# A squared-ReLU MLP whose last 96 hidden units move from three matmuls a tile to two and a packed quarter

## The chip, the cores and the metric

The kernel runs on one core of a Trainium2 chip. The metric is the device time of one execution in microseconds. Engines are named as in the profile: PE is TensorE (PEld its weight loads), DVE VectorE, ACT ScalarE, POOL GpSimd, and SP is SyncE, which here only issues transfers (its queue shows as SPq).

## The reference

One block of a transformer with two branches in parallel on 2048 tokens of 512 features, in float32:

```python
x = A_x                                   # [1, 2048, 512]
xn = layernorm(x)                         # no weights
# A: linear attention, 32 heads of 16
q, k, v = (xn @ wqkv) split into heads    # wqkv [512, 1536]
phi = lambda t: where(t > 0, t + 1, exp(t)) + 1e-6
kv = einsum("bhsd,bhse->bhde", phi(k), v) # over all tokens, not causal
z = einsum("bhsd->bhd", phi(k))
o = einsum("bhqd,bhde->bhqe", phi(q), kv) / (phi(q) . z + 1e-6)
A = o @ wo                                # wo [512, 512]
# B: an MLP of 1376 hidden units
h = relu(xn @ w1 + b1) ** 2               # w1 [512, 1376]
B = h @ w2 + b2                           # w2 [1376, 512]
return x + A + B
```

The 1376 hidden units are ten chunks of 128 and a last one of 96. That last chunk, number 10, is what the change is about.

## The kernel before

**Numbers.** TensorE multiplies operands in a rounded format (`fp32r`). To keep float32 accuracy every operand is held as a pair: the rounded value, called high, and the rest, called low, which is the difference between the value and its high part. ScalarE writes the high part with a copy (L109), VectorE subtracts for the low part (L117, L120). A product of two pairs is three matmuls into one accumulator, high·high, high·low and low·high: the helper `three`, whose matmul is L128, goes through

```python
PASSES = ((0, 0), (0, 1), (1, 0))
```

**Tokens.** 2048 tokens are 16 tiles of 128, in four blocks of four tiles. All tiles are read once for the layer norm, the keys and the attention sums. Then two pairs of blocks are worked, n = 0 (blocks 3 and 2) and n = 1 (blocks 1 and 0). `t1` is the first block of a pair, `t2` the second.

**A pair of blocks.** The hidden units of chunks 0 to 9 are made in pairs of chunks, for both blocks at once, by a scheme with seven products in place of eight (`product`, L453), in steps p = 0 to 4 and a closing one, p = 5. Chunk 10 stands alone: `plain_1` computes it for block `t1` ahead of step 0 and for block `t2` inside step 0. The hidden values of `t1` are used while the steps run: `mlp_2` (L457) multiplies the hidden values of a chunk, 128 tokens at a time, with the rows of `w2` of that chunk, three matmuls a tile, into four PSUM accumulators `acc`. The hidden values of `t2` are kept in the tiles `r2a` to `r2c` and used after the steps, in "the second block" (L1036 to L1095). `add_attention` adds the attention's product with `wo` for one tile (`aTsr`, `aTsra` are pairs of the transposed attention result, made by a transpose `at` on VectorE, L285, from `g`, which transfers have regrouped in memory). `add` (L903) then adds the accumulator on VectorE to `res`, the rows of `x` loaded by `load_res` (L893), and `store` writes the result out.

**Chunk 10 and b2.** Chunk 10 has 96 rows of `w1` columns and `w2` rows. `raw_1` (L175) and `piece_2` (L193) fill the other 32 by a memset on GpSimd, and `b2` is loaded as row 96 of the `w2` tile. The bias `b1` of unit 96 is 1 and its weights are 0, so its hidden value is 1 and `b2` enters through the matmul that has to be done anyway. In the first block of a pair chunk 10 is the first to enter `acc` (step 0); in the second it is one of `last_two`, the two chunks whose products come after the attention's (`sum_2`, L998). The last tile of all is done in two halves of 256 columns, `end`, so that its sum and store can begin earlier.

**Order.** The order is written by hand (`manual_schedule`): the instructions of each engine run in the order in which the program names them. An instruction that waits holds all that stands behind it on its engine. All transfers are issued by SyncE in program order as well: one whose buffer is not free yet, or whose source is not written yet, holds those behind it. Loads of weights go into a ring of six raw buffers of 128x512 float32 (`raw`), from which ScalarE and VectorE make the pairs. The same ring holds the temporary sums `S1` and `S3` of `chunk_sums` (L696 to L705).

`piece_2` issues the load and returns two pieces of work, the copy and the subtraction, which `next_2` (L871) or `do(w2next, 2)` puts in later; `next_2` keeps the `w2` of the next chunk one step ahead. In the second block, the loop over the chunks (L1036) runs over nine chunks, e = 0 to 8; at e it multiplies chunk `waiting[e]`, makes the hidden pair for a later one (`wait_for`, L994), puts in the pieces of `w2` loaded before and loads the `w2` of `waiting[e + 8]`, so that chunk 10, the last in `waiting`, is loaded at e = 2, just ahead of `load_res(t2)`. At e = 3, in the pair n = 0 alone, a megabyte of normalised tokens for the next pair is loaded (`xt`, L1043); then come the `wqkv` rows for the next queries (`rq`, L162; their pairs `wrh`, `wrl`). Between them `move(4)` issues the transfers `g` that regroup the attention result.

Of the kernel before, what the change touches and what calls it, by code (L numbers as in the profile page):

```python
# [13 lines left out]
P = 128  # L14
# [4 lines left out]
def kernel(  # L19
# [46 lines left out]
    assert D == 512 and S % BT == 0 and FL % 32 == 0 and FL < P  # L66
# [79 lines left out]
    ident = keep.tile([P, P], F32, name="ident")  # L146
    heads = work.tile([P, P], F32, name="heads", tag="heads")
    b1s = keep.tile([P, NF], F32, name="b1s")
    zb = keep.tile([P, D], F32, name="zb")
# [10 lines left out]
    def raw(name, src):  # L160
        t = w512(name, "raw", 6)
        nc.sync.dma_start(t[:, :src.shape[-1]], src)  # L162
        return t
# [10 lines left out]

    def raw_1(f):  # L175
        n = min(P, F - f * P)
        t = w512(f"r1_{f}", "raw", 6)
        tj = t.rearrange("p (j n) -> p j n", j=NJ)
        if n < P:
            nc.gpsimd.memset(tj[:, :, n:], 0.0)  # L180
        nc.sync.dma_start(tj[:, :, :n], w1[:, f * P:f * P + n].rearrange("(j p) n -> p j n", j=NJ))
        return t
# [10 lines left out]
    def piece_2(f, at):  # L193

        if f < NF - 1:
            t = raw(f"r2_{f}", w2[f * P:(f + 1) * P, :])
        else:
            t = w512(f"r2_{f}", "raw", 6)
            nc.gpsimd.memset(t[FL:, :], 0.0)  # L199
            nc.sync.dma_start(t[:FL, :], w2[f * P:, :])  # L200
            nc.sync.dma_start(t[FL:FL + 1, :], b2[None, :])
        w2s[f] = [w2r[at // 2][:, at % 2 * 2 + u] for u in range(2)]
        h, l = w2s[f]
        return [lambda: copy("act", h, t), lambda: rest_of(l, t, h)]
# [234 lines left out]

    def relu(o, i, f):  # L440
# [16 lines left out]
    def mlp_2(acc, f, s, first=False):  # L457
        for k in range(TB):
            three(acc[k], [s[:, u, k * P:(k + 1) * P] for u in range(2)], w2s[f], first, False)

# [31 lines left out]
    nc.gpsimd.memset(b1s[:, NF - 1:], 0.0)  # L492
    nc.gpsimd.memset(b1s[FL:FL + 1, NF - 1:], 1.0)
# [126 lines left out]
    def less_last(j):  # L620
        if j == 0:
            nc.sync.dma_start(wvs, wqkv[:, 2 * D:].rearrange("(j p) d -> p j d", j=NJ))
            w = w512("wvl", "raw", 6)
# [23 lines left out]
    for i in range(2, NT):  # L647
        if i == NPE:
            wq = both("wq", ("B0", "B1"))
        if i == 3:  # L650
            nc.sync.dma_start(b1s[:, :NF - 1], b1[:(NF - 1) * P].rearrange("(f p) -> p f", p=P))
            nc.sync.dma_start(b1s[:FL, NF - 1:], b1[(NF - 1) * P:, None])
# [43 lines left out]
    def chunk_sums(n, t):  # L696

        (a11, a12), (a21, a22) = ((x[:, 0], x[:, 1]) for x in t)
        sa, sb = (w512(f"S{k}_{n}", "raw", 6).rearrange("p (c n) -> p c n", c=2) for k in (1, 3))
# [90 lines left out]
    for n in range(2):  # L790
# [76 lines left out]
        s = {NF - 1: hidden_2(f"sz{n}", rz)}  # L867
# [23 lines left out]
        t5, res = None, {}  # L891

        def load_res(t):  # L893
            for k in range(2):
# [3 lines left out]
                for i in range(2):  # L898
                    res[t, 2 * k + i] = r[:, i, :]

# [8 lines left out]
        for p in range(NP + 1):  # L909
# [6 lines left out]
            if p:  # L916
                nc.vector.tensor_tensor(out=t5, in0=before, in1=t5, op=OP.add)
            if 0 < p < NP:
                chunk_split(1, 0, s34)
            if p:  # L920
                relu(r2[fb - 2], t5, fb - 2)
            if p < NP:
# [22 lines left out]
            if p == 0:  # L945
                T.update({k: tokens_sum(k, f"B{k - 3}") for k in (3, 4)})
                def last_sums(k):
                    for f in (difference_high, difference_low):
# [3 lines left out]
                last_sums(3)  # L952
# [5 lines left out]
            else:  # L958

                plain_1(before, z, x2)  # L960
                relu(r2[NF - 1], before, NF - 1)
            s[fa] = hidden_2(f"s{n}_{fa}", c11)
# [4 lines left out]
            if p + 2 < NP:  # L967
                w = load_1(p + 2)
            product(A, S2, [T[2][:, u] for u in range(2)])
# [9 lines left out]
            if p == 0:  # L979
                last_sums(4)  # L980
            relu(r2[fa], c12, fa)
            next_2(2 * p + 2)
            if p:
                mlp_2(acc, fb - 2, s.pop(fb - 2))
            else:
                mlp_2(acc, NF - 1, s.pop(NF - 1), True)
# [49 lines left out]
        for e, f in enumerate(waiting[:-2]):  # L1036
# [28 lines left out]
        for k in range(TB):  # L1065
            add_attention(acc, t2 * TB + k, n == 1 and k == last)
# [47 lines left out]
```

## Time and profile before

The median of three runs is 422.51 us (422.31 to 422.54).

| | |
|---|---|
| profiled execution, its own time | 422.49 us |
| its span in the trace | 420.8 us |
| TensorE busy | 415.2 us, 99% of the span, 1860 matmuls |
| VectorE busy | 294.2 us, 70%, 536 instructions |
| ScalarE busy | 254.0 us, 60%, 451 instructions |
| GpSimd busy | 27.6 us, 7%, 50 instructions |
| transfers | 46.16 MB, mean 110 GB/s |
| granted TensorE clock | 1.000 |
| 128x512 matmul, mean duration in the records | 389 ns |

A row of the groups of instructions names the line, the engine, the operation, the output and the inputs by their names in the program, the shape, and the count; then busy time and mean duration of one, and the idle time of the engine just ahead of such instructions with what ended most of it. Matmuls are pipelined, so the durations of neighbours overlap: 1860 matmuls of up to 389 ns fit into 415 us. GpSimd works in the first quarter of the span, apart from a few small memsets. The 40 slices of the page show TensorE at 9 tenths or more from the second slice to the last but one, with the granted clock at full throughout.

### The profile page before, as it was taken

Reading aid. Unit: us, or ns where it says so; the run is one execution under the profiler, and the core shown is the slowest. Engines: PE = TensorE matmul, PEld = TensorE weight load, DVE = VectorE, ACT = ScalarE, POOL = GpSimd, SP = SyncE. Lnnn points to the kernel's source line nnn. Section 1 sums busy time; section 2 is a strip of 40 time slices with the busy share of each in tenths; the row PEclk is TensorE's granted clock in tenths of the full one; section 3 lists DMA queues with packets and bytes.
Section 4 is the critical chain, followed back from the end, with each engine's and each line's share of the span. In section 5 each row is a group of like instructions: output and inputs, shape, how many; then the busy total and the mean of one; then the engine's idle time right before and its main releaser. Section 6 shows DMA issues by size and latency. Waiting matters only on the chain.

```text
span 420.8 us, 5373 instructions
## 1 busy us (share of the span) xinstructions
PE 415.2 (99%) x1860; PEld 343.6 (82%) x1860; DVE 294.2 (70%) x536; ACT 254.0 (60%) x451; POOL 27.6 (7%) x50
## 2 busy tenths in 40 slices
PE   7999999999999999999999999999999999999996
PEld 7788888888887888888888888888888888888885
DVE  6886767777578877677579475586967667577343
ACT  5867777675467767665457362676667665546230
POOL 3242222220000000000000000000000000000000
PEclk9999999999999999999999999999999999999999
DMA  7885422800412231645026652401120654024502
GB/s 240 286 243 157 130 89 92 278 15 3 112 50 77 75 100 26 199 82 169 0 85 191 173 196 97 124 0 50 51 75 25 202 101 149 2 95 97 152 0 100
DMA packets 44818, 46.16 MB, mean 110 GB/s; under 512 B 5716, under 2 KB 31060, under 8 KB 44536
## 3 DMA queue, kind: packets, MB, share of 16 engines
q1 hardware_dynamic: 44792, 45.84, 36.5%
q8 instruction: 14, 0.23, 0.2%
q14 instruction: 12, 0.10, 0.1%
HBM read 32.71 MB, written 8.91 MB: 99 GB/s over the span
## 4 chain that ended last, share of the span: by engine, by line
PE 98%; DVE 1%; DMA 1%; ACT 0%; issue 0%
PE acc L128 39%; PE b L453 23%; PE kx L380 10%; PE pk L361 10%; PE pq L361 10%; PE pz L128 1%; PE b L128 1%; PE pkv L773 1%; PE pm L128 1%; DMA x<-in_A_x_dram 1%; PE pt L300 1%; PE end L128 0%; DVE st L214 0%; DVE xp L253 0%; DVE res L903 0%; ACT xs1h L316 0%
## 5 line engine op out<-in xcount | busy, mean ns | idle before, releaser
L128 PE MATMUL acc<-w2r,s 128*128 128x512 f32 x498 | 116.6, 389 | 0.0
L128 PEld LDWEIGHTS acc<-w2r,s 128*128 128x128 f32 x498 | 93.5, 188 | 19.6
L453 PE MATMUL b<-T,aop 128*128 128x512 f32 x240 | 59.6, 389 | 0.0
L453 PEld LDWEIGHTS b<-T,aop 128*128 128x128 f32 x240 | 45.0, 188 | 9.4
L380 PE MATMUL kx<-pk,tok 128*128 128x512 f32 x192 | 46.8, 392 | 0.0
L380 PEld LDWEIGHTS kx<-pk,tok 128*128 128x128 f32 x192 | 35.6, 188 | 7.9 <-DVE pk L369 0.6
L128 PE MATMUL acc<-mh,aTsr 128*128 128x512 f32 x96 | 30.3, 390 | 0.0
L109 ACT ACTIVATE w2r<-r 128x512 fp32r<-128x512 f32 x32 | 20.0, 625 | 13.8 <-PE acc L128 11.3
L120 DVE TENSOR_TENSOR w2r<-r,w2r 128x512 fp32r<-128x512 f32 x32 | 21.9, 685 | 7.3 <-ACT w2r L109 7.2
L453 PE MATMUL b<-xs0h,aop 128*128 128x512 f32 x80 | 26.4, 391 | 0.0
L117 POOL TENSOR_TENSOR tok<-xp,tok 128x512 fp32r<-128x512 f32 x16 | 21.7, 1362 | 54.9 <-ACT tok L109 54.9
L117 DVE TENSOR_TENSOR s<-c,s 128x512 fp32r<-128x512 f32 x20 | 13.8, 692 | 16.3 <-ACT s L109 16.3
L356 DVE SCALAR_TENSOR_TENSOR q<-pq,q 128x512 f32<-128x512 f32 x16 | 11.0, 689 | 14.9 <-ACT q L354 14.9
L109 ACT ACTIVATE aop<-S 128x512 fp32r<-128x512 f32 x20 | 12.6, 629 | 14.6 <-DVE S L702 9.4
L128 PEld LDWEIGHTS acc<-mh,aTsr 128*128 128x128 f32 x96 | 18.0, 188 | 3.8
L903 DVE TENSOR_TENSOR res<-acc,res 128x512 f32<-128x512 f32 x16 | 11.0, 692 | 14.2 <-PE acc L128 14.2
L352 ACT ACTIVATE q<-pq 128x512 f32<-128x512 f32 x16 | 9.4, 591 | 18.5 <-PE pq L361 18.5
L199 POOL MEMSET r<- 32x512 f32 x3 | 1.6, 522 | 278.2 <-DVE w2r L120 272.3
L128 PE MATMUL acc<-ml,aTsr 128*128 128x512 f32 x48 | 18.7, 390 | 0.0
L453 PEld LDWEIGHTS b<-xs0h,aop 128*128 128x128 f32 x80 | 15.0, 188 | 3.4 <-ACT rz L441 0.3
L453 PE MATMUL b<-xs0l,aop 128*128 128x512 f32 x40 | 15.6, 389 | 0.0
L285 DVE STREAM_TRANSPOSE at<-g 128x512 f32<-128x512 f32 x16 | 10.5, 689 | 6.8 <-DMA g<-q 6.8
(192 smaller groups left out, 826.7 us busy)
## 6 DMA issues: line engine op xcount, KB each, us to landing
r<-in_B_w_dram SPq DMA_DIRECT2D x49, 256.0 KB, 3.2
res<-in_A_x_dram SPq DMA_DIRECT2D x8, 512.0 KB, 5.9
g<-q SPq DMA_DIRECT2D x64, 64.0 KB, 2.1
out_dram<-res SPq DMA_DIRECT2D x15, 256.0 KB, 2.1
x<-in_A_x_dram SPq DMA_DIRECT2D x5, 512.0 KB, 5.6
via<-xp SPq DMA_DIRECT2D x5, 512.0 KB, 2.6
xg<-via SPq DMA_DIRECT2D x20, 128.0 KB, 3.0
xTd<-t SPq DMA_DIRECT2D x8, 256.0 KB, 3.1
```

Of the source, the lines that this page charges most:

```text
L109: nc.scalar.activation(o, i, AF.Copy, bias=bias)
L117: ENG[el].tensor_tensor(out=l, in0=src, in1=f32(h), op=OP.subtract)
L120: nc.vector.tensor_tensor(out=l, in0=src, in1=f32(h), op=OP.subtract)
L128: nc.tensor.matmul(ps, lhsT=a[u], rhs=b[v], start=first and n == 0, stop=last and n == 2)
L285: nc.vector.transpose(o.rearrange("p j (r t) -> p r j t", r=NJ), G.rearrange("p r (j c) -> p r j c", j=NJ))
L300: nc.tensor.transpose(t[k][:, at:at + P], xp[i][:, j * P:(j + 1) * P], ident)
L352: nc.scalar.activation(p, ps, AF.Relu, scale=-1.0)
L356: nc.vector.scalar_tensor_tensor(p, ps, 0.0, p, op0=OP.max, op1=OP.add)
L361: nc.tensor.matmul(ps, lhsT=cols(i)[u][:, j, slot(i)], rhs=w[v][:, j, :], start=first and n == 0, stop=last and n == len(steps) - 1)
L380: nc.tensor.matmul(kxp[c], lhsT=tok[i][:, u, c * P:(c + 1) * P], rhs=pk[i][:, v], start=i == 0 and (u, v) == first, stop=i == NT - 1 and ( ...
L453: nc.tensor.matmul(ps, lhsT=a[u][:, j * P:(j + 1) * P], rhs=b[v][:, j, :], start=first and j == 0 and n == 0, stop=last and j == 1 and n == 2,
L903: nc.vector.tensor_tensor(out=r[:, a:z], in0=ps, in1=r[:, a:z], op=OP.add)
```

## The change

Chunk 10's 96 units are laid out over 128 rows. `units(f)` says which: rows 0 to 63 hold units 32 to 95 of the chunk, and rows 64 to 95 and 96 to 127 both hold units 0 to 31. High and low parts of different units then share a tile, so that two matmuls of 128 rows (`last_2`) cover all but one 32-row product per token tile, and that one is done for the four tiles of a block together (`quarters_2`): four matmuls of 32 rows, each in another quarter of the rows of the array and into another accumulator. `b2` no longer has a row; GpSimd's queue adds it to `res` by accumulating transfers (`add_bias`).

What else moves: in the pair n = 0, step 0, the subtractions for chunk 10's hidden part stand later (`sz_rests`), and the last one of `T`'s pieces and a `next_2` move into step 1; the ring has five raw buffers, not six; in the second block chunk 10's load stands at e = 3, behind `load_res(t2)`, the `g` transfers of that step and, in the pair n = 0, `xt`; the two `wait_for` at the end of the second block change places. On GpSimd the memsets are gone, and copies of 64x512 and 32x512 come in their place. SyncE issues three transfers for each chunk-10 load.

```diff
     w2s, wos = {}, {}
-    ident = keep.tile([P, P], F32, name="ident")
+    ident = keep.tile([P, P], F32, name="ident", tag="ident")
     heads = work.tile([P, P], F32, name="heads", tag="heads")
     b1s = keep.tile([P, NF], F32, name="b1s")
-    zb = keep.tile([P, D], F32, name="zb")
+    w2q = keep.tile([P, D], F32R, name="w2q")
+    zb = work.tile([P, D], F32, name="zb")
     eps = keep.tile([P, 1], F32, name="eps")
...
     def raw(name, src):
-        t = w512(name, "raw", 6)
+        t = w512(name, "raw", 5)
         nc.sync.dma_start(t[:, :src.shape[-1]], src)
...
+    def units(f):
+        if f < NF - 1:
+            return [(0, f * P, P)]
+        return [(0, f * P + Q, 2 * Q), (2 * Q, f * P, Q), (3 * Q, f * P, Q)]
     def raw_1(f):
-        n = min(P, F - f * P)
-        t = w512(f"r1_{f}", "raw", 6)
+        t = w512(f"r1_{f}", "raw", 5)
         tj = t.rearrange("p (j n) -> p j n", j=NJ)
-        if n < P:
-            nc.gpsimd.memset(tj[:, :, n:], 0.0)
-        nc.sync.dma_start(tj[:, :, :n], w1[:, f * P:f * P + n].rearrange("(j p) n -> p j n", j=NJ))
+        for a, o, n in units(f):
+            nc.sync.dma_start(tj[:, :, a:a + n], w1[:, o:o + n].rearrange("(j p) n -> p j n", j=NJ))
         return t
...
+        h, l = w2s[f] = [w2r[at // 2][:, at % 2 * 2 + u] for u in range(2)]
         if f < NF - 1:
             t = raw(f"r2_{f}", w2[f * P:(f + 1) * P, :])
-        else:
-            t = w512(f"r2_{f}", "raw", 6)
-            nc.gpsimd.memset(t[FL:, :], 0.0)
-            nc.sync.dma_start(t[:FL, :], w2[f * P:, :])
-            nc.sync.dma_start(t[FL:FL + 1, :], b2[None, :])
-        w2s[f] = [w2r[at // 2][:, at % 2 * 2 + u] for u in range(2)]
-        h, l = w2s[f]
-        return [lambda: copy("act", h, t), lambda: rest_of(l, t, h)]
+            return [lambda: copy("act", h, t), lambda: rest_of(l, t, h)]
+        t = w512(f"r2_{f}", "raw", 5)
+        for a, o, n in units(f):
+            nc.sync.dma_start(t[a:a + n], w2[o:o + n, :])
+        def high():
+            copy("act", h, t)
+            copy("pool", l[2 * Q:], h[:2 * Q])
+            for k in range(TB):
+                copy("pool", w2q[k * Q:(k + 1) * Q], h[2 * Q:3 * Q])
+        def low():
+            rest_of(l[:2 * Q], t[:2 * Q], h[:2 * Q])
+            rest_of(h[3 * Q:], t[3 * Q:], h[3 * Q:])
+        return [high, low]
...
+    def hidden_last(name, r):
+        nc.scalar.activation(r, r, AF.Square)
+        s = pair(name)
+        h, hl = s[:, 0], s[:, 1]
+        lq = keep.tile([P, P], F32R, name=f"{name}q", tag="ident")
+        copy("act", h, r)
+        copy("pool", hl[:2 * Q], h[:2 * Q])
+        def rests():
+            rest_of(hl[2 * Q:], r[:2 * Q], h[:2 * Q])
+            for k in range(TB):
+                at, to = slice(2 * Q, 3 * Q), slice(k * P, (k + 1) * P)
+                rest_of(lq[k * Q:(k + 1) * Q], r[at, to], h[at, to])
+        return (h, hl, lq), rests
     def relu(o, i, f):
...
+    def last_2(ps, k, s, first, stop, a=0, z=D):
+        for u in range(2):
+            nc.tensor.matmul(ps, lhsT=s[u][:, k * P:(k + 1) * P], rhs=w2s[NF - 1][u][:, a:z],
+                             start=first and u == 0, stop=stop and u == 1)
+    def quarters_2(acc, s):
+        for k in range(TB):
+            at = slice(k * Q, (k + 1) * Q)
+            nc.tensor.matmul(acc[k], lhsT=s[2][at], rhs=w2q[at], start=False, stop=False)
     def add_attention(acc, i, last=False):
...
                                 channel_multiplier=sign)
-    nc.gpsimd.memset(b1s[:, NF - 1:], 0.0)
-    nc.gpsimd.memset(b1s[FL:FL + 1, NF - 1:], 1.0)
     groups = {}
...
             nc.sync.dma_start(b1s[:, :NF - 1], b1[:(NF - 1) * P].rearrange("(f p) -> p f", p=P))
-            nc.sync.dma_start(b1s[:FL, NF - 1:], b1[(NF - 1) * P:, None])
+            for a, o, n in units(NF - 1):
+                nc.sync.dma_start(b1s[a:a + n, NF - 1:], b1[o:o + n, None])
         move()
...
         (a11, a12), (a21, a22) = ((x[:, 0], x[:, 1]) for x in t)
-        sa, sb = (w512(f"S{k}_{n}", "raw", 6).rearrange("p (c n) -> p c n", c=2) for k in (1, 3))
+        sa, sb = (w512(f"S{k}_{n}", "raw", 5).rearrange("p (c n) -> p c n", c=2) for k in (1, 3))
         for o, x, y, op in ((sa[:, 0], a21, a22, OP.add), (sa[:, 1], sa[:, 0], a11, OP.subtract),
...
         relu(rz, ps, NF - 1)
-        s = {NF - 1: hidden_2(f"sz{n}", rz)}
+        sz, sz_rests = hidden_last(f"sz{n}", rz)
+        s = {}
+        if n:
+            sz_rests()
...
         r2 = {f: r2[k // 4][:, k % 4] for k, f in enumerate(waiting)}
-        t5, res = None, {}
+        t5, res, biased = None, {}, []
...
                     res[t, 2 * k + i] = r[:, i, :]
+                biased.append(r)
+        def add_bias():
+            def to(r):
+                for i in range(2):
+                    nc.gpsimd.dma_start(r[:, i], b2[None, :].partition_broadcast(P), accum_op=OP.add)
+            todo = [lambda r=r: to(r) for r in biased]
+            biased.clear()
+            return todo
...
                 nc.vector.tensor_tensor(out=t5, in0=before, in1=t5, op=OP.add)
+            if p == 1:
+                last_sums(4, difference_low)
             if 0 < p < NP:
...
                 relu(r2[fb - 2], t5, fb - 2)
+            if p == 1:
+                next_2(2)
             if p < NP:
...
                 T.update({k: tokens_sum(k, f"B{k - 3}") for k in (3, 4)})
-                def last_sums(k):
-                    for f in (difference_high, difference_low):
+                def last_sums(k, *what):
+                    for f in what:
                         for j in range(2):
...
-                last_sums(3)
+                last_sums(3, difference_high, difference_low)
             if p or n:
...
                 relu(r2[NF - 1], before, NF - 1)
+                if n == 0:
+                    sz_rests()
             s[fa] = hidden_2(f"s{n}_{fa}", c11)
...
                 w = load_1(p + 2)
+            if p == NP - 1:
+                do(bias, 2)
             product(A, S2, [T[2][:, u] for u in range(2)])
...
             if p == 0:
-                last_sums(4)
+                last_sums(4, difference_high)
             relu(r2[fa], c12, fa)
-            next_2(2 * p + 2)
             if p:
+                next_2(2 * p + 2)
                 mlp_2(acc, fb - 2, s.pop(fb - 2))
             else:
-                mlp_2(acc, NF - 1, s.pop(NF - 1), True)
+                for k in range(TB):
+                    last_2(acc[k], k, sz, True, False)
+                quarters_2(acc, sz)
             if p == TB - 1:
...
                 load_res(t1)
+            if p == 3:
+                bias = add_bias()
         def wait_for(f):
-            s[f] = hidden_2(f"s{n}_{t2}_{f}", r2[f])
+            name = f"s{n}_{t2}_{f}"
+            if f < NF - 1:
+                s[f] = hidden_2(name, r2[f])
+            else:
+                s[f], rests = hidden_last(name, r2[f])
+                rests()
         def sum_2(acc, k, f, first, stop, a=0, z=D):
+            if f == NF - 1:
+                last_2(acc, k, s[f], first, stop, a, z)
+                return
             three(acc, [s[f][:, u, k * P:(k + 1) * P] for u in range(2)],
...
                 do(w2next, 2)
-                if e + 8 < NF:
-                    g = waiting[e + 8]
+                k = e + 8 if e < 2 else e + 7
+                if k < NF and e != 2:
+                    g = waiting[k]
                     w2next.extend(piece_2(g, place(g)))
...
                 load_res(t2)
+            if e == 4:
+                bias = add_bias()
+            if e in (6, 7):
+                do(bias)
             if 0 < e < 5:
...
         for k in range(TB):
+            if n == 1 and k == last:
+                quarters_2(acc, s[NF - 1])
             add_attention(acc, t2 * TB + k, n == 1 and k == last)
             if k < 2:
-                wait_for(last_two[k])
+                wait_for(last_two[1 - k])
                 pieces(1)
...
             add(acc[last], t2, last)
+        else:
+            quarters_2(acc, s[NF - 1])
         for k in range(TB):
```

More of the change, by code (lines that the diff above doesn't have):

```diff
@@ L65 @@
     FL = F - (NF - 1) * P
-    assert D == 512 and S % BT == 0 and FL % 32 == 0 and FL < P
+    Q = P // TB
+    assert D == 512 and S % BT == 0 and FL == 3 * Q
     nc.scalar.preload_act_table_set("natural_log_exp_and_others")
@@ L622, in less_last @@
             nc.sync.dma_start(wvs, wqkv[:, 2 * D:].rearrange("(j p) d -> p j d", j=NJ))
-            w = w512("wvl", "raw", 6)
+            w = w512("wvl", "raw", 5)
             nc.sync.dma_start(w, wqkv[D - 1:, 2 * D:].partition_broadcast(P))
```

## Prediction

> **What bounds the kernel now.** I read the page first, then the chain in order of time, then who waits for whom, then the timelines around the places that the diff touches.
>
> ```profile
> span 420.8 us, 5373 instructions
> ...
> PE 415.2 (99%) x1860; PEld 343.6 (82%) x1860; DVE 294.2 (70%) x536; ACT 254.0 (60%) x451; POOL 27.6 (7%) x50
> ```
>
> The span, and each engine's busy time. The chain that ended last, by engine:
>
> ```profile
> PE 98%; DVE 1%; DMA 1%; ACT 0%; issue 0%
> ```
>
> Two rows of the groups of instructions (count, busy time, mean ns of one, idle time ahead of them):
>
> ```profile
> L128 PE MATMUL acc<-w2r,s 128*128 128x512 f32 x498 | 116.6, 389 | 0.0
> L128 PEld LDWEIGHTS acc<-w2r,s 128*128 128x128 f32 x498 | 93.5, 188 | 19.6
> ```
>
> TensorE carries 98% of the chain, so a matmul removed is time won, unless TensorE then waits. A matmul's 389 ns overlap their neighbours'; what one costs is its pitch, from the chain in order of time (start, length, engine, output, line, how many):
>
> ```profile
> 138.19 2.72 PE acc L128 x12
> ```
>
> 512 columns: 2.72/12 = 0.2267 us a matmul. At the very end, 256 columns, 1.44/12 = 0.120:
>
> ```profile
> 416.03 1.44 PE end L128 x12
> ```
>
> And 128 columns, with a new weight tile for each:
>
> ```profile
> 108.36 3.57 PE pkv L773 x32
> ```
>
> 3.57/32 = 0.1116; that is the closest row to the pace of weight loads.
>
> **The change, part by part.**
>
> *Matmuls.* The last chunk costs three matmuls for each of 16 token tiles; now two. The last tile is done in two halves, so what goes is 15 × 0.2267 + 2 × 0.120 = 3.64 us. Four groups of four 32-row matmuls come in, each of the four in its own row group, with its own 128-column weight load and 512 columns. No row shows one. Lower bound of a group: all four stream together, 0.227. Upper bound in a dense stream: one after the other, 4 × 0.2267 = 0.907, at which removing and adding cancel (3.64 − 3.63). I take the pace of `pkv` for the loads: the first is hidden under the matmul ahead as every load is now, three more take 3 × 0.1116, then the last streams its 0.2267: 0.56 a group, 2.25 in all. Gain 3.64 − 2.25 = **1.39** (ends 2.73 and 0.01; with drains, below, a loss).
>
> The Trainium skill (TensorE: Matmul & The Clock Gate, Part 3: Packing small matmuls) reports 3.07 times for four row tiles of 512 columns; by it a group would be 0.907/3.07 = 0.30 and the gain 2.46, an estimate.
>
> *The first block's start.* Chunk 10's two subtractions on VectorE (hidden and weights) become seven: the weights' two at once, the hidden part's 64-row one and four 32x128 ones later, after `T`.
>
> ```profile
> 131.52 0.68 DVE L117 TENSOR_TENSOR sz<-rz,sz 128x512 fp32r<-128x512 f32 x1
> 135.20 1.30 DVE L120 TENSOR_TENSOR T<-Tf,T 128x512 fp32r<-128x512 f32 x2 [1.20 <-ACT T L109]
> 138.03 2.88 PE L128 MATMUL acc<-w2r,sz 128*128 128x512 f32 x12
> ```
>
> And, from further on, a VectorE instruction of half the columns:
>
> ```profile
> 183.58 0.42 DVE L702 TENSOR_TENSOR S<-r,S 128x256 f32<-128x256 f32 x1
> ```
>
> Fewer rows save nothing, the columns count: the weights' pair takes two slots of 0.6 there. Behind `T` (136.5) come 0.60 for the 64 rows and some 0.25 for each quarter (the last row has 256 columns in 0.42, the first 512 in 0.68): 137.1 and 138.1. TensorE wants the first at 138.26 and the quarters after eight matmuls, at 139.8. That leaves 1.1 us against GpSimd, which now copies (next part). Price 0 to 1.2; I take 0.3.
>
> *GpSimd copies.* Five copies for each weight load of chunk 10 and one for each hidden part replace the memsets. Without a row of their own they lie between a 512-column memset and a two-input subtraction:
>
> ```profile
> L117 POOL TENSOR_TENSOR tok<-xp,tok 128x512 fp32r<-128x512 f32 x16 | 21.7, 1362 | 54.9 <-ACT tok L109 54.9
> L199 POOL MEMSET r<- 32x512 f32 x3 | 1.6, 522 | 278.2 <-DVE w2r L120 272.3
> L117 DVE TENSOR_TENSOR wql<-rq,wqh 128x512 fp32r<-128x512 f32 x4 | 4.0, 1044 | 0.6 <-ACT wqh L109 0.6
> L120 DVE TENSOR_TENSOR w2r<-r,w2r 128x512 fp32r<-128x512 f32 x32 | 21.9, 685 | 7.3 <-ACT w2r L109 7.2
> ```
>
> And from the timelines of GpSimd and VectorE (start, length, operation, in brackets the idle time ahead and what ended it), where the two meet:
>
> ```profile
> 73.57 1.33 POOL L117 TENSOR_TENSOR tok<-xp,tok 128x512 fp32r<-128x512 f32 x1 [4.06 <-ACT tok L109]
> 74.05 2.01 DVE L117 TENSOR_TENSOR wql<-rq,wqh 128x512 fp32r<-128x512 f32 x2 [0.30 <-ACT wqh L109]
> ```
>
> Two VectorE subtractions that met a GpSimd subtraction took 2.01 instead of some 1.3; `wql` averages 1044 ns where its like take 685. So GpSimd off the path still delays VectorE, by up to its own remaining time.
>
> *b2 by transfers.* Sixteen accumulating transfers on GpSimd's queue, 256 KB each, take the place of a row that cost no matmul. They follow `res` loads, many microseconds ahead of the additions; GpSimd's program order, not TensorE, times them. I cost them at nothing, except where they meet other transfers below.
>
> *Five raw buffers for six.* Loads now wait for a later release; the worst in both block pairs is `r2_8`, which waits for the last chunk sums (the row at 183.58, above) and stands ahead of 16 `g` transfers.
>
> ```profile
> 179.34 10.95 SPq L281 DMA_DIRECT2D g<-q  x16
> 197.20 0.62 ACT L109 ACTIVATE w2r<-r 128x512 fp32r<-128x512 f32 x1
> 199.85 0.73 ACT L441 ACTIVATE r2a<-c,b1s 128x512 f32<-128x512 f32 x1 [2.02 <-DVE c L977]
> 202.75 1.29 DVE L285 STREAM_TRANSPOSE at<-g 128x512 f32<-128x512 f32 x2
> ```
>
> The `g` issues move from 179.3–190.3 to about 184.5–195.5, and land some 2 us later, still ahead of 202.75. `r2_9`, queued behind them, comes some 1.3 us late for ACT's copy at 197.2, which has 2.02 idle behind it. Cost 0; if the cover went, ACT would be that late.
>
> *The second block's last weights: the decisive edit.* SyncE's queue issued chunk 10's weights ahead of `res`. Now they stand behind `xt`, a megabyte, in the same queue. `xt` itself waits until all `g` have landed.
>
> ```profile
> 232.32 0.53 SPq L200 DMA_DIRECT2D r<-in_B_w_dram  x1
> 233.24 0.90 SPq L897 DMA_DIRECT2D res<-in_A_x_dram  x2
> 234.19 2.55 SPq L281 DMA_DIRECT2D g<-q  x4
> 240.88 0.35 SPq L1043 DMA_DIRECT2D xt<-xTd  x1
> 241.33 2.06 SPq L162 DMA_DIRECT2D rq<-in_A_wqkv_dram  x4
> ```
>
> These are SyncE's issues (start, length of issuing, line, output and source, how many). Then ScalarE, VectorE and TensorE in the same stretch:
>
> ```profile
> 242.81 0.62 ACT L109 ACTIVATE w2r<-r 128x512 fp32r<-128x512 f32 x1
> 244.90 0.63 ACT L109 ACTIVATE aTsr<-at 128x512 fp32r<-128x512 f32 x1 [1.47 <-DVE at L285]
> 246.42 0.63 ACT L109 ACTIVATE wrh<-rq 128x512 fp32r<-128x512 f32 x1 [0.89 <-DMA rq<-in_A_wqkv_dram]
> 248.43 0.63 ACT L109 ACTIVATE aTsr<-at 128x512 fp32r<-128x512 f32 x1 [1.38 <-DVE at L285]
> 248.97 0.61 ACT L109 ACTIVATE wrh<-rq 128x512 fp32r<-128x512 f32 x1
> ```
>
> ```profile
> 243.56 0.68 DVE L120 TENSOR_TENSOR w2r<-r,w2r 128x512 fp32r<-128x512 f32 x1
> 244.16 0.70 DVE L285 STREAM_TRANSPOSE at<-g 128x512 f32<-128x512 f32 x1
> 247.08 0.69 DVE L117 TENSOR_TENSOR wrl<-rq,wrh 128x512 fp32r<-128x512 f32 x1 [2.22 <-ACT wrh L109]
> 247.69 0.71 DVE L285 STREAM_TRANSPOSE at<-g 128x512 f32<-128x512 f32 x1
> 248.32 1.47 DVE L120 TENSOR_TENSOR aTsr<-at,aTsr 128x512 fp32r<-128x512 f32 x2
> ```
>
> ```profile
> 250.15 0.62 PE L128 MATMUL acc<-mh,aTsr 128*128 128x512 f32 x2
> ```
>
> ACT's copy of the chunk-10 weights (242.81) stands in both orders ahead of `aTsr`, and VectorE's subtraction ahead of the transpose `at`; the attention matmul at 250.15 needs their low half, ready today near 248.97. Now the load takes the place of the first `rq`, which ended ACT's wait at 246.42, or 5.54 after `xt`'s issue. Two issues fewer ahead of `res` bring `xt` 0.92 forward (232.32 to 233.24); the accumulating transfers that start when `res` has landed hold it back by 0 to 1.4 (512 KB beside what is still under way). I take 0.6: `xt` at 240.6, weights at **246.1** (ends 245.5, 247.0) instead of long before 242.81.
>
> From there by the rows' distances: subtraction +0.75, its new second half +0.60, transpose +0.60, `aTsr` +0.74, `wrh` +0.54 (ACT's spacing of copies, 248.43 to 248.97), `wrl` +0.66, second transpose +0.61, low half +0.63, its length 0.69: 5.82, so 251.9. With some 0.25 for the weight load the matmul of 250.15 starts at 252.2: a stall of 2.0. The five GpSimd copies start with the same event and hold VectorE by 0 to 0.85; I take 0.4. **Stall 2.4** (ends 1.4 and 3.8). The last block has no `xt`, and its weights come in time.
>
> *Sum.* −1.39 + 0.3 + 2.4 = +1.3. The profiled execution took 422.49 (420.8 span, 1.7 around), beside a median of 422.51: **423.8**.
>
> **Rivals.**
>
> *Hidden, and faster.* If the chunk-10 weights land by about 244 (the 16 engines serving small transfers beside `xt` rather than behind it), the stall is under the gain; with no stall at all, 422.49 − 1.39 = 421.1. The turning point is a landing near 244.7 to 245.2. Against it: `rq`, in the same place, ended its wait only at 246.42.
>
> *The row groups do not run side by side.* Then a group costs 0.907, nothing is won, and the stalls stay: 422.49 + 2.7 = 425.2. The change would not do what it says.
>
> *Drains.* Entering and leaving a 32-row group, TensorE might run empty: the tail 0.389 − 0.227 = 0.16, a bare load 0.188, three more at 0.1116, a whole matmul 0.389, a bare load 0.188: 1.26 a group, 5.04 for 3.64: 1.4 lost, and 426.6 with the stalls. No matmul in the trace changes its row count, so no row speaks for or against. The Trainium skill (TensorEngine Tiling (Array Packing), Tiling Modes, Key Properties) says that changing the tiling mode drains TensorE; no run shown so far bears on that.
>
> **How the numbers follow.** About 0.2% (0.85 us: 421.65 to 423.35) is what tells a change from none. Stall larger than gain, as summed: 0.60, own range 422.8 to 425.4, of it 0.13 within 0.2%. Hidden: 0.22, of it 0.15 faster. No packing: 0.10, of it 0.01 within. Drains: 0.08. So slower 0.64, same 0.21, faster 0.15. The range reaches from the hidden case (421.1) to near the drain case: 421.1 to 426.2; what lies outside is the lower end of the hidden case and the upper part of the drains.
>
> **What would show it.** Matmul count unchanged at 1860 less 17 plus 16, 1859. Four groups reading `w2q`: starts within 0.12 of each other and 0.56 to the next full matmul prove the packing; 0.227 apart the second rival; gaps of 0.35 ahead of and behind them the drains. In the wait view ACT's `w2r` waits 2 to 4 us for a transfer near 246, and TensorE for `aTsr` around 250. If TensorE is still 99% busy with no such wait, the stall was wrong; if TensorE waits near 138 for `sz`, the first block's price was too small.

## The result and the profile after

The changed kernel takes 429.37 us (median of five runs, 429.19 to 430.79), the kernel before 422.54 beside it: 1.0161 times as long, 95% interval 1.0135 to 1.0186. Forecast was 423.8, in a range of 421.1 to 426.2. The direction was right, the size was not, and the time lies outside the range.

The profiled execution of the changed kernel took 430.79 us, the slowest of the five, with a span of 429.1. Its page:

```profile
span 429.1 us, 5471 instructions
...
PE 418.5 (98%) x1859; PEld 343.1 (80%) x1859; DVE 304.1 (71%) x555; ACT 253.7 (59%) x451; POOL 54.8 (13%) x78
...
PEclk9999999999999999999999987999999999999999
```

TensorE's busy time rose by 3.3 us with one matmul fewer, and the row of the granted clock, all 9s before, has an 8 and a 7 in two slices past the middle, around 260 us. TensorE's waits:

```profile
PE acc L129 <- ACT aTsr L110: 2.5, 1, 2.5
PE acc L129 <- DVE aTsr L121: 2.1, 1, 2.1
...
PE acc L500 <- DVE sz L121: 0.8, 1, 0.8
```

(us in total, times, longest). The two waits for `aTsr` are at the place that the prediction named, and the one for `sz` is in the first block. The chain in order of time shows how the delay grew. Its rows of before at three marks (a full step after the first block, the queries behind the second block, the last addition), then of after:

```profile
155.87 6.80 PE b L453 x30
...
260.79 21.76 PE pq L361 x96
...
417.50 0.42 DVE res L903
```

```profile
157.00 6.80 PE b L489 x30
...
269.39 21.76 PE pq L379 x96
...
425.62 0.42 DVE res L964
```

The delay is 1.13 after the first block, 8.60 after the second, and 8.12 at the last addition; 0.2 more at the very end makes the 8.3 between the spans. So the first block lost 1.13, the second block of n = 0 lost 7.47, and the two blocks of n = 1 together won 0.48. The changed kernel profiled a second time (429.65 us, `after_again` below) has the first two marks at 156.36 and 268.28: there the first block lost 0.49 and the second 7.00. The sizes that follow are those of one execution, the slower of the two.

**The second block of n = 0.** First the end of the chain that leads to the second wait (start, length, what):

```profile
241.92 7.58 DMA r<-in_B_w_dram
...
249.66 0.64 ACT w2r L110
...
251.03 1.01 DVE w2r L121
...
253.97 1.07 DVE wrl L118
...
256.29 3.78 PE acc L129 x8
```

In full this is the forecast path link by link: weights, subtraction, transpose, `aTsr`, `wrh`, `wrl`, transpose, low half, matmul. It took 6.6 from the copy of the weights to the matmul, as against 6.5 forecast (6.1 and 0.4 for GpSimd). GpSimd, copying all the while, cost rather 0.7: the two VectorE rows shown took 1.01 and 1.07, and 0.68 and 0.69 before. Only its start was late: the last part of the weights landed at 241.92 + 7.58 = 249.5, not 246.1. Before the wait, `xt` (240.23, forecast 240.6) and the weights had been issued in the order forecast, and with them ran the first b2 transfers (issue queues of SyncE and GpSimd):

```profile
240.23 0.34 SPq L1124 DMA_DIRECT2D xt<-xTd  x1
240.63 1.74 SPq L210 DMA_DIRECT2D r<-in_B_w_dram  x3
```

```profile
237.61 1.74 POOL L956 DMA_DIRECT2D res<-in_B_b_dram  x2 [54.55 <-DMA res<-in_A_x_dram]
```

From its issue to its landing `xt` took 7.6 us, 4.8 in the kernel before. Then the clock, by stretches of time (busy time and count of each engine, granted clock, DMA share, GB/s):

```profile
254.00:255.00 1.00, 0.20 (x1) 0.00 (x0) 1.00 (x2) 0.00 (x0) 1.00 (x3) 1.00 0.00 0
255.00:261.00 6.00, 4.71 (x11) 3.74 (x12) 5.33 (x12) 5.24 (x10) 2.25 (x3) 0.50 0.49 87
261.00:262.00 1.00, 1.00 (x4) 0.77 (x4) 1.00 (x3) 1.00 (x3) 0.00 (x0) 0.57 0.00 0
```

From 255.0 on the granted clock is half, and it stays so until nearly 262. The twelve matmuls from 256.29 to 261.58 took 5.29 us, 0.44 each; at 0.2267 they would have taken 2.72. That is 2.6 us that nobody waited for and that no row of waits shows. Together: the matmul that would have started at 250.83 + 2 x 0.2267 = 251.28 (0.2267 behind the last one at 250.60, and the third of its tile) started at 256.29, 5.0 late; 5.0 + 2.6 is the second block's loss but for 0.1, its packing gain of 0.24 set against it.

**The packed matmuls.** A group in the second pair, on TensorE's timeline:

```profile
303.23 1.97 PE L500 MATMUL acc<-w2r,sz 128*128 128x512 f32 x8
305.14 0.51 PE L507 MATMUL acc<-w2q,sz1q 32*128 32x512 f32 x4
305.57 1.65 PE L489 MATMUL b<-T,aop 128*128 128x512 f32 x6
307.07 0.39 PE L489 MATMUL b<-xs0h,aop 128*128 128x512 f32 x1
```

Four matmuls of some 495 ns each lie within 0.51 us: they start within 0.02 of each other. From the eight's start to the last row are 3.84 us, of which fourteen full matmuls are 3.17: a group costs 0.67. It starts 0.10 late behind the eight, takes 0.43 to the next start, and the matmuls behind it lose another 0.14.

**The first block.** ScalarE and VectorE near 135 us:

```profile
135.10 0.63 ACT L110 ACTIVATE w2r<-r 128x512 fp32r<-128x512 f32 x1 [3.04 <-DMA r<-in_B_w_dram]
```

```profile
137.38 1.29 DVE L121 TENSOR_TENSOR T<-Tf,T 128x512 fp32r<-128x512 f32 x2 [0.92 <-ACT T L110]
138.71 0.69 DVE L121 TENSOR_TENSOR sz<-rz,sz 64x512 fp32r<-64x512 f32 x1
139.42 1.22 DVE L121 TENSOR_TENSOR sz0q<-rz,sz 32x128 fp32r<-32x128 f32 x4
```

ScalarE stood 3.0 us for chunk 0's rows of `w2`; `T`, behind that copy, ended 2.2 later than before, and `sz`, which now stands behind `T`, is late for the matmul that wanted it at 138.6. It is not GpSimd that holds it: its copies ended at 135.8, and the five subtractions take 0.69 and 0.31 each.

### The profile page after: what moved, and what is told of

It is laid out like the page before. It is cut to its first block, busy times and chain, and to the rows that moved or that the text cites. A ratio compares the mean times of both kernels' runs of the same rounds, so it can differ in the third digit from the quotient of the medians.

```text
span 429.1 us, 5471 instructions
## 1 busy us (share of the span) xinstructions
PE 418.5 (98%) x1859; PEld 343.1 (80%) x1859; DVE 304.1 (71%) x555; ACT 253.7 (59%) x451; POOL 54.8 (13%) x78
## 4 chain that ended last, share of the span: by engine, by line
PE 88%; DMA 4%; DVE 4%; ACT 1%; SPq 1%; issue 1%; DVEq 0%; ACTq 0%
PE acc L129 31%; PE b L489 21%; PE kx L398 10%; PE pk L379 10%; PE pq L379 10%; DMA r<-in_B_w_dram 3%; PE acc L500 2%; SPq L299 1%; PE pkv L820 1%; DMA g<-q 1%; DMA x<-in_A_x_dram 1%; PE b L129 1%; PE pz L129 1%; PE pt L318 1%; DVE at L303 0%
## 5 line engine op out<-in xcount | busy, mean ns | idle before, releaser
L129 PE MATMUL acc<-w2r,s 128*128 128x512 f32 x477 | 112.7, 389 | 0.0
L129 PEld LDWEIGHTS acc<-w2r,s 128*128 128x128 f32 x477 | 89.5, 188 | 18.9 <-issue 0.2
L956 POOL DMA_DIRECT2D res<-in_B_b_dram x16 | 14.1, 1066 | 200.7 <-DVE w2r L121 55.2
L129 PE MATMUL acc<-mh,aTsr 128*128 128x512 f32 x96 | 32.8, 416 | 4.6 <-ACT aTsr L110 2.5
L121 DVE TENSOR_TENSOR w2r<-r,w2r 128x512 fp32r<-128x512 f32 (+2 forms) x35 | 24.9, 713 | 16.4 <-ACT w2r L110 16.2
L129 PEld LDWEIGHTS acc<-mh,aTsr 128*128 128x128 f32 x96 | 19.3, 202 | 9.8 <-ACT aTsr L110 2.9
L129 PE MATMUL acc<-ml,aTsr 128*128 128x512 f32 x48 | 19.7, 410 | 0.0
L387 DVE SCALAR_TENSOR_TENSOR pk<-k,pk 128x512 fp32r<-128x512 f32 x16 | 11.6, 727 | 4.3 <-PE kx L398 2.3
## 6 DMA issues: line engine op xcount, KB each, us to landing
r<-in_B_w_dram SPq DMA_DIRECT2D x49, 256.0 KB, 3.5
res<-in_B_b_dram POOLq DMA_DIRECT2D x16, 256.0 KB, 5.5
out_dram<-res SPq DMA_DIRECT2D x15, 256.0 KB, 2.1
```

The lines of the kernel that those rows point to most:

```text
L121: nc.vector.tensor_tensor(out=l, in0=src, in1=f32(h), op=OP.subtract)
L129: nc.tensor.matmul(ps, lhsT=a[u], rhs=b[v], start=first and n == 0, stop=last and n == 2)
L387: nc.vector.scalar_tensor_tensor(pk[i][:, 1], p, 1e-6, f32(pk[i][:, 0]), op0=OP.add, op1=OP.subtract)
L956: nc.gpsimd.dma_start(r[:, i], b2[None, :].partition_broadcast(P), accum_op=OP.add)
```

## The experiments

The theory after the first look: (A) the transfers that add b2 run beside `xt` and hold it and chunk 10's weights back; TensorE then empties and loses half its clock; in the first block the smaller ring delays a load. The rival (B): the place of the load behind `xt` is the whole cause, and the b2 transfers are incidental. All medians below stand beside the kernel before at 422.5 to 422.6 on the same chip.

**No b2 transfers.**

```diff
-                for i in range(2):
-                    nc.gpsimd.dma_start(r[:, i], b2[None, :].partition_broadcast(P), accum_op=OP.add)
+                pass
```

> The changed kernel without its sixteen accumulating transfers; b2 is left out of the sum. Theory A, the transfers that accumulate b2 into res hold back xt and with it chunk 10's weights near 240 us of the pair n = 0: xt lands about 4.8 us after its issue and no longer 7.6, the weights near 246.5 and not 249.5, TensorE's two waits for aTsr shrink from 4.6 us together to 2 or less. 423.5 to 424.5 if TensorE then keeps its clock, some 426.5 if it drops to half all the same. Rival B, the place of the load behind xt is what costs and the accumulating transfers are incidental: 428.5 to 429.4.

427.03 us (425.02 to 429.78). ScalarE's copy of the weights in the profiled execution (425.12 us):

```profile
246.32 0.63 ACT L110 ACTIVATE w2r<-r 128x512 fp32r<-128x512 f32 x1 [4.36 <-DMA r<-in_B_w_dram]
```

The weights are there at 246.3, 3.3 sooner, and one wait for `aTsr` of 1.6 is left. That is A in its place, and nearly the 246.1 of the prediction, which counted 0.6 for these transfers. The two executions at full granted clock (1.000, 0.999) took 425.1 and 425.0, over A's 424.5; the three at 0.995 or 0.996 took 427.0, 427.4 and 429.8, the last as slow as rival B. Those three were not profiled: how long TensorE waited in them is not known.

**Chunk 10's load ahead of xt.**

```diff
+            if n == 0 and e == 3:
+                f2 = xT[t2 - 2] = four(f"xt{t2 - 2}", "r3")
+                nc.sync.dma_start(f2, xTd[t2 - 2])
             if e == 2:
                 load_res(t2)
```

(the same three lines are taken out further up, ahead of chunk 10's load)

> The changed kernel, with chunk 10's load issued ahead of xt in the pair n = 0, the accumulating transfers where they are. Theory A: ScalarE no longer waits for chunk 10's weights (they land by 243), but xt still lands late, and rq behind it near 250, so that ScalarE waits for rq, and the low half of aTsr is late by some 2 us: 424 to 425.5, the clock kept. Rival B, the order alone decides: the whole loss of that place is gone, 421.7 to 422.2.

423.71 us (422.98 to 424.64; ratio 1.0025, 1.0014 to 1.0035): the low end of A's forecast, missed by 0.3, and not B's. ScalarE's timeline shows where the wait went:

```profile
242.74 0.63 ACT L110 ACTIVATE w2r<-r 128x512 fp32r<-128x512 f32 x1 [0.20 <-DMA r<-in_B_w_dram]
...
249.73 0.63 ACT L110 ACTIVATE wrh<-rq 128x512 fp32r<-128x512 f32 x1 [3.23 <-DMA rq<-in_A_wqkv_dram]
```

The weights are in time, and `rq`, behind the late `xt`, is late in their stead; TensorE waits 0.7 for `aTsr`.

**Matmuls in the gap.**

```diff
+    def idle(ps, k):
+        for _ in range(k):
+            nc.tensor.matmul(ps, lhsT=m[0][:, 0, :P], rhs=m[0][:, 0, :], start=True, stop=True)
...
+        if spare is not None:
+            idle(spare, 8)
...
+                    if q == 2:
+                        idle(spare, 6)
```

> The changed kernel with 14 extra matmuls on a spare accumulator where TensorE stands idle near 250 us of the pair n = 0: eight ahead of the first matmul with aTsr, six ahead of the first that needs its low half (8 x 0.227 = 1.8 us into a gap of 2.6, 6 x 0.227 = 1.4 into one of 2.2). Clock theory: the granted clock drops to half because TensorE stood idle, so with the gaps filled it stays at 1.00, the twelve matmuls after the gap run at 0.227 and not 0.44, and the time falls by 2.3 to 2.7, to about 426.8. Rival, these matmuls were slow for their operands' or another engine's sake: no change, 429.2 to 430.

The same stretches of time as above:

```profile
254.00:255.00 1.00, 0.88 (x4) 0.75 (x5) 0.38 (x1) 0.59 (x2) 0.94 (x2) 1.00 0.00 0
255.00:261.00 6.00, 5.28 (x24) 4.03 (x23) 5.32 (x11) 4.59 (x9) 2.89 (x4) 1.00 0.54 87
```

The clock stays at 1.00, and the six microseconds that held 11 matmuls hold 24. From the mark after the first block to the queries are 267.42 - 157.51 = 109.91, 2.5 less than the 112.39 of the changed kernel: within the forecast. Of the two profiled executions the one with fillers took 1.9 less (428.89 against 430.79), since its first block lost 0.5 more, which the fillers don't touch. The medians are only 0.65 apart (428.72 against 429.37), so the forecast of 426.8 was missed. So that the half clock follows from idleness is shown by the stretch and by the clock of all four executions (0.999 to 1.000), and its price in the whole time only in part.

**Chunk 0's w2 loaded first.**

```diff
+        if n == 0:
+            early[0] = raw("r2_0", w2[:P, :])
         w = load_1(1)
...
-            t = raw(f"r2_{f}", w2[f * P:(f + 1) * P, :])
+            t = early.pop(f, None) or raw(f"r2_{f}", w2[f * P:(f + 1) * P, :])
```

> The changed kernel, in the pair n = 0 with the load of chunk 0's rows of w2 issued ahead of the two loads of w1 that wait for a raw buffer. Ring theory: the wait of ScalarE for these rows (3.0 us at 132 us) goes, VectorE's subtraction for sz is back near 137, and TensorE's gap of 0.94 at 138.6 closes: 428.4. Rival, GpSimd's new copies hold VectorE and sz stays late: less than 0.3 won, 429.1 to 429.4.

The gap is gone on TensorE's timeline:

```profile
138.51 1.99 PE L502 MATMUL acc<-w2r,sz 128*128 128x512 f32 x8
```

Yet the time is 429.84, no better. TensorE came to the second block earlier and waited there for the same transfers: 3.0 and 1.6 for `aTsr` in place of 2.5 and 2.1. The expectation had the place right and forgot that a later wait swallows an earlier gain.

**The changed kernel again, and the moves one on top of the other.**

> The changed kernel once more, beside the next three on the same chip. All theories: 429.2 to 430.2, TensorE at half clock for some 6 us after its gap near 250 us.

429.38 us. TensorE behind its first wait for `aTsr` in the profiled execution, and the clock in stretches of time:

```profile
253.11 0.79 PE L129 MATMUL acc<-mh,aTsr 128*128 128x512 f32 x1 [2.76 <-ACT aTsr L110]
```

```profile
250.50:253.00 2.50, 0.00 (x0) 0.00 (x0) 1.87 (x3) 0.57 (x2) 2.32 (x4) 1.00 0.07 24
253.25:259.75 6.50, 4.90 (x11) 3.41 (x12) 5.50 (x10) 4.68 (x9) 3.58 (x5) 0.50 0.47 81
```

Here the clock is at half as soon as the first wait, of 2.8 us, is over. Then the b2 transfers alone moved behind GpSimd's copies:

```diff
-            if e in (6, 7):
+            if e in (6, 7) if n else e in (7, 8):
                 do(bias)
```

> The changed kernel; in the pair n = 0 the accumulating transfers of the second block start behind GpSimd's copies of chunk 10's weights, so that none runs beside xt. Chunk 10's load stays behind xt. Theory A: xt lands about 5.4 after its issue as in the kernel without these transfers, the weights near 246.3, TensorE waits 1.5 to 2.5 for aTsr; 424.5 to 425.5 where its clock holds, 427 to 428 where it drops. Rival, the later transfers take the same time from rq and nothing is won: 428.5 to 429.5.

425.53 us (424.84 to 427.42), three executions at a granted clock of 0.999 or 1.000 from 424.8 to 425.9 and one at 0.996 with 427.4, as A had both cases. One wait of 1.7 for `aTsr` is left. Moving the transfers in time does what leaving them out did.

Chunk 10's load ahead of `xt` as well:

> The changed kernel with both: chunk 10's load ahead of xt, and the accumulating transfers behind GpSimd's copies. Theory A: no wait for aTsr is left, and what remains is the first block's gap of some 1.3 less the packing's 0.97: 422.6 to 423.1. Rival, rq is held back by the moved transfers and TensorE still waits 1 to 2 near 250: 424 to 425.

422.91 us (422.13 to 423.30, without one execution that took 463.37 at a granted clock of 0.852); no wait for `aTsr` is left. And chunk 0's rows first:

> As both_moved, and chunk 0's rows of w2 loaded ahead of the two w1 loads in the first block. Theory: nothing is left but the packing, four groups at 0.24 each: 421.3 to 421.7. Rival, the gap of the first block comes back in another place (the w1 loads, now later): 422.5 or more.

421.62 us, 0.9981 of before (0.9972 to 0.9990). Now the same move of chunk 0's rows, worth nothing above, is worth 1.3. Its page, with TensorE's share of the chain at 97% again, and the first two marks:

```profile
span 419.7 us, 5471 instructions
...
PE 97%; DMA 1%; ACT 0%; SPq 0%; DVE 0%; issue 0%
```

```profile
155.40 6.80 PE b L491 x30
...
260.01 21.76 PE pq L381 x96
```

The second block takes 104.61 us between these marks, 104.92 before. All that the change lost lay in the order of transfers; with the three moves it is faster than the kernel before, by its packing.

**What a group costs.** On top of the three moves, first all four matmuls of a group in one row group:

```diff
-            at = slice(k * Q, (k + 1) * Q)
+            at = slice(0, Q)
```

> The kernel with all three moves, and all four 32-row matmuls of a group in the first row group (the first tile's low parts stand in for the other three tiles', so what is summed is another product; the counts and shapes stay). Theory, the four run side by side because their row groups differ: here they run one after the other, a group takes about 0.67 + 3 x 0.227 = 1.35 and not 0.67, four of them 2.7 more: 424.0 to 424.6. Rival, row groups do not matter (short matmuls overlap anyway): 421.4 to 421.9.

424.54 us, 2.92 more, 0.73 a group where the theory had 0.68:

```profile
297.56 1.20 PE L509 MATMUL acc<-w2q,sz1q 32*128 32x512 f32 x4
```

1.20 us in place of 0.51: they run one after the other. Then without them:

```diff
-        for k in range(TB):
-            at = slice(k * Q, (k + 1) * Q)
-            nc.tensor.matmul(acc[k], lhsT=s[2][at], rhs=w2q[at], start=False, stop=False)
+        return
```

> The kernel with all three moves and without the sixteen 32-row matmuls, whose products are left out of the sum. Theory, a group costs 0.67 as the starts around it show: 4 x 0.67 = 2.7 less, 418.8 to 419.1. Rival, pure streaming, 0.227 a group and the rest an artefact of the records: 420.7. Rival, drains of 1.26 a group: 416.6.

419.15 us, 2.47 less than with them: 0.62 a group, beside the 0.67 of the starts. These two ran on another chip than the kernel with the three moves, with the kernel before at 422.57 beside them and not 422.48; against it the two prices are 0.71 and 0.64.

**What makes the b2 transfers dear.** In the changed kernel, writing over in place of adding; and plain transfers of the same size from different rows:

```diff
-                    nc.gpsimd.dma_start(r[:, i], b2[None, :].partition_broadcast(P), accum_op=OP.add)
+                    nc.gpsimd.dma_start(r[:, i], b2[None, :].partition_broadcast(P))
```

> The changed kernel, with the sixteen transfers of b2 writing over res in place of adding to it (x is left out of the sum); same bytes moved, same places. Theory, accumulating is what makes them dear, for the old value has to be read as well: xt takes about 6.5 us from issue to landing and not 7.6 to 8.5, the weights land a microsecond or two earlier, 426.5 to 428. Rival, the bytes written alone count: 429.0 to 429.8.

```diff
-                    nc.gpsimd.dma_start(r[:, i], b2[None, :].partition_broadcast(P), accum_op=OP.add)
+                    nc.gpsimd.dma_start(r[:, i], xf[(2 * i + 1) * P:(2 * i + 2) * P, :])
```

> The changed kernel, with the sixteen transfers of b2 replaced by plain transfers of the same size from 128 different rows of x (neither b2 nor the right rows of x are in the sum). Theory, one row of 2 KB read 128 times is what holds the transfer engines: xt lands 5.5 to 6.5 after its issue, 425 to 428. Rival, 256 KB each beside xt are dear whatever they read: xt takes 7.5 to 9 as with b2, 429 to 431.5.

431.11 us and 428.07 us. The row of GpSimd's queue on the pages of the changed kernel, of the one that writes over, and of the one with different rows (packets, MB, share of the 16 engines' span):

```profile
q0 software_dynamic: 2304, 4.20, 6.2%
```

```profile
q0 software_dynamic: 1280, 4.20, 4.9%
```

```profile
q0 software_dynamic: 1280, 4.20, 3.2%
```

An eighth of these, the 512 KB beside `xt`, is 0.062 x 429.1 / 8 = 3.3 us of all sixteen engines, then 2.6, then 1.7: estimates, from the mean of the sixteen transfers. The theory that adding is what makes them dear fell: writing over was no faster in time, and ScalarE's copy of the weights began at 249.76 with it, 249.66 in the changed kernel. Reading one row of 2 KB for all 128 partitions is dearer than reading 128 rows, by 0.9 of those 3.3; adding takes another 0.7. But the time with different rows is only 1.3 less than with b2, between the two expectations; in its profiled execution `xt` took less to land, but was itself issued 1.3 later than in the changed kernel. Why writing over took 1.7 longer than adding is open.

**Five buffers in the kernel before.**

```diff
-        t = w512(name, "raw", 6)
+        t = w512(name, "raw", 5)
```

(and at the other places that name the ring)

> The kernel before with five raw buffers for six. Theory, the smaller ring alone is covered, for in the old order sz and the chunk-10 weights are ready ahead of the late load: 422.4 to 422.7. Rival, the late load of chunk 0's rows of w2 stops TensorE in this order too: 423.2 or more.

423.09 us (422.43 to 423.22), ratio 1.0009 (1.0000 to 1.0018): between the two. ScalarE and TensorE in the first block:

```profile
134.87 0.63 ACT L109 ACTIVATE w2r<-r 128x512 fp32r<-128x512 f32 x1 [2.73 <-DMA r<-in_B_w_dram]
```

```profile
138.20 2.89 PE L128 MATMUL acc<-w2r,sz 128*128 128x512 f32 x12
```

With five buffers ScalarE waits 2.7 for chunk 0's rows in the old order too, but `sz` is ready and the matmuls with it run without a gap. The ring alone costs 0.5 (0 to 0.8); what the first block lost beyond that needs the moved subtractions as well. They alone, with six buffers, were not run.

## Why the prediction was wrong

Its sum against the profiled execution, in us:

| term | forecast | measured |
|---|---|---|
| packing, four groups | -1.39 (-2.73 to -0.01) | 4 x -0.24 = -0.96 |
| first block's start | +0.3 (0 to 1.2) | 1.13 + 0.24 = +1.4 |
| wait in the second block, n = 0 | +2.4 (1.4 to 3.8) | +5.0 |
| half clock behind that wait | not in the sum | +2.6 |
| end | 0 | +0.2 |
| sum | +1.3 | +8.2; the spans differ by 8.3 |

Of the 6.9 by which the sum is off, 2.6 are the size of the wait, 2.6 the clock, 1.1 the first block, 0.4 the packing and 0.2 the end. The medians are only 6.8 apart, as this execution was the slowest; in the nine profiled executions with this first block the first mark lies between 156.36 and 157.51, which makes its price 0.7 to 1.9.

*Right.* The deciding edit, its place, the queue order and the path of nine links: 6.6 measured, 6.5 forecast (5.9 and 0.7 for GpSimd, forecast 6.1 and 0.4, so the sum is closer than its parts). The hidden case's price (no wait left, 421.1) is close to the kernel with all three moves, 421.62, though it counted on 0.4 more from the packing; its condition, the landing by about 244, is what chunk 10's load ahead of `xt` makes true. The row groups do run side by side, so that rival is out: one row group costs 0.7 more a group. The drain rival is out by size: 0.67, not 1.26. That the last block has cover held too.

*Wrong, first: "hold it back by 0 to 1.4".* This step priced 512 KB of b2 as bytes of any kind and put the price on the issue of `xt`. But `xt` was issued at 240.23, ahead of the forecast 240.6; it was its landing that was late, 7.6 after the issue, as against 5.5 without the b2 transfers. They occupied the sixteen engines for 3.3 us by the estimate above and put off ScalarE's copy of the weights by 3.3 (246.32 without them, 249.66 with). GpSimd issued them as soon as `res` had landed, 237.61, ahead of `xt`. That the weights without them came near 246.1 is in part luck, for the 246.1 held 0.6 for them.

*Wrong, second: a stall was priced as idle time alone.* The page of before shows the clock at 9s throughout, and the forecast had no case in which it changes. The runs show 2.6 us behind the wait, and a clock that stays where the gaps are filled. By quarter-microsecond stretches the half clock lasted 6.8 us here (255.0 to 261.9), 6.8 in the second profile of the changed kernel (253.1 to 260.0) and 3.4 with the transfers from different rows (256.0 to 259.4). It fell 4.0 us after the last dense matmul here, though two single ones had run in between, and in the second profile at the end of the first wait, 2.8 long. The Trainium skill (TensorE: Matmul & The Clock Gate, Part 1: The HAM clock gate) states that TensorE runs at half clock after about one idle window of 3.4 us and needs about as long of work to come back, and that the window runs freely. The traces agree with the half (0.50) and with a length of one or two such windows; they differ in the idle time, of which 2.8 us were enough. The rule was on a page of the Trainium skill that the prediction cited for something else, and it would have given a rival with a chance of its own, as the forecast wait reached to 3.8.

*Wrong, third: "Cost 0" for five raw buffers.* The step looked for the worst wait and named `r2_8`. That one was hidden: the delay is 1.13 at 157.00, and 1.13 still at the start of the second block. The load that was late was chunk 0's, behind two loads of `w1` in SyncE's queue, and what made it count was the other edit, which puts `sz` behind `T` and so behind that copy; the kernel before with five buffers has the same late load, and no gap. Each of the two was judged with the cover that the other took away. GpSimd, which the 0.3 was for, had no part in it.

*Mis-sized: a group.* 0.56 forecast, 0.62 to 0.67 measured. The weight loads are not what it pays for, since all four start together; it pays 0.10 ahead, 0.20 in the group beyond the 0.227, and 0.14 behind. The Trainium skill's 3.07 (TensorE: Matmul & The Clock Gate, Part 3: Packing small matmuls), 0.30 a group by estimate, is not what the kernel gets: one lonely group between full matmuls reaches 0.907 / 0.67 = 1.35. The Trainium skill (TensorEngine Tiling (Array Packing), Tiling Modes, Key Properties) says that a change of mode drains TensorE; the 0.10 and the 0.14 at the group's two ends may be that, which no run separates, and are much smaller than the drain rival had them.

## What to carry to other kernels

Where a wait of TensorE is forecast, price the clock with it: matmuls that started 5.0 us late cost 7.6 here. Put a small load ahead of a large one in the same queue, and start transfers that nobody waits for after the ones that somebody does; three such moves turned 429.4 into 421.6 without touching the arithmetic. Judge edits that share a cover together, and expect an early gain to vanish into a later wait until that wait is gone.

## What the hardware showed unexpectedly

- 4.2 MB that read one 2 KB row for 128 partitions held the sixteen transfer engines for 4.9% of the span, the same bytes from different rows for 3.2%, and added to the destination from one row for 6.2%.
- The half clock lasted 6.8 us in both profiled executions of the changed kernel and 3.4 with the transfers from different rows, and once began at the end of a single wait of 2.8 us. Whether a wait of 1.6 or 1.7 is enough is not shown: the executions of such kernels at 0.995 or 0.996 were not profiled, and one of the kernel before (424.09 us) also ran at 0.996.
- Four 32-row matmuls started within 0.02 us of each other, without any of the weight-load pace that the 128-column matmuls show (0.1116); in one row group the four took 1.20 and not 0.51.
